# Retention block and gated MLP in one kernel: residual of all pairs through DMA transposes, small work moved to VectorE and GpSimd, and another written order

## The chip, the core and the metric

The kernel runs on one core of a Trainium2 chip. The metric is the device time of one launch in microseconds. The kernel before took 213.18 us, the median of three runs (212.71 to 213.91). One more execution was taken by the hardware profiler; its numbers are below.

## The reference

Two blocks, one after the other, for a batch of 8 sequences of 576 positions.

```
# 1: retention, 8 heads of 64
scores = (q @ k.T) / sqrt(64)
ret    = scores * Dmat            # Dmat[h,i,j] = gamma[h]**(i-j) for i >= j, else 0
x      = ret @ v                  # heads side by side: x is (8, 576, 512)
# 2: gated MLP
h      = gelu_tanh(x @ w_in)      # 512 -> 1024
u, vv  = h[..., :512], h[..., 512:]
v_n    = (vv - mean) / sqrt(var + 1e-6) * g_ln
v_s    = einsum('ts,bsd->btd', w_sg, v_n) + b_sg[:, None]
out    = x + (u * v_s) @ w_out    # fp32
```

Inputs and outputs are fp32; the kernel computes in bf16 with fp32 sums.

## The kernel before

Two sequences make a pair, and there are four pairs (p = 0 to 3). The 1152 rows of a pair are nine tiles of 128 rows, numbered i = 9p + m; the middle one (m = 4) holds the last 64 rows of both sequences. Retention works in five blocks per pair, b = 5p + n: four of 256 rows of one sequence and one of the 64 + 64 last rows.

For each block, q, k and v are loaded as fp32 (lines 338 and 341). q and v are multiplied by powers of gamma and cast to bf16 (line 384, tiles `qb`, `vb`); k is cast only (lines 372 and 374, `kb`). q and k are transposed on TensorE against the identity, either 128 rows wide (line 420) or as two concurrent 64-row halves (line 430), and copied out of PSUM (lines 253 and 254, `qT`, `kT`). In the last pair the q and k of the four 256-row blocks are transposed by four DMAs instead (line 455). Scores are matmuls (line 486), masked on VectorE while they leave PSUM (lines 499 and 502, `ret`). The state of earlier blocks is a sum of k-v products (`zp`, line 522; `run` and `zb`, lines 547 to 556). The output (line 568) lands transposed, as x's columns, in `xT`, copied there by ScalarE or VectorE (lines 253 and 254).

The MLP takes `xT` as its weights or its moving operand. Per tile: `hv` (four matmuls, line 642), gelu on ScalarE (line 649, `vg`), mean and variance on VectorE (lines 657 and 658), then four small GpSimd operations in `m_rs` (lines 662 to 665: add epsilon, power -1/2, product with the mean, sign), then the norm on ScalarE (line 677, `vn`; line 674 for the middle tile, which is written in two halves to `vmid`). `hu` (line 692) and its gelu (line 703, `uT`) need only `xT`. For each sequence, `wp` (line 713) multiplies four column groups of `vn` with the transposed w_sg (ten matmuls each), and VectorE multiplies the result into `uT` (line 723). Finally `op` (line 745) multiplies `uT` with w_out, the residual is added, and the 128 rows are stored (lines 771 and 774).

The residual x has to be in row order, but `xT` holds columns. The constant XP = 1 says which pairs do what: for p < XP, four more matmuls of `xT` against the identity go into the same PSUM tile ahead of the product (line 740), and ScalarE copies the sum out (line 760). For p >= XP, a DMA transpose on SP's queue writes the rows to `xr` (line 754; five buffers), and VectorE adds it while it evacuates (line 762).

Nothing is scheduled by the machine or by a planner: every piece of work is a job with a number, and the string ORDER lists all jobs. The program is emitted in that order, so each engine's queue is the list filtered by its engine. Job numbers follow from the loops that create the jobs; a letter after a number picks another engine (P, D, A, G; F is the wide form of the transposes). A token f16, f12 or f4 adds that many 128-column matmuls on a zero tile `warm`, merged into calls of up to 512 columns, at the head of the next PSUM tile (line 231). There are eight such tokens, 76 units, all in the first seventh of the list. All loads, stores and DMA transposes are issued by SP in list order, and SP waits at an entry whose source or buffer isn't ready; there are eight `ld` buffers and two of `ldq`.

The first jobs on each engine: TensorE turns the small vectors into columns (line 780), does f16, block 0's transposes, two groups of row transposes (line 803), f12, block 0's scores and state, f12, block 1's transposes, f4, block 0's output, block 1's scores, f4, `hv` of tiles 0 and 1, f12. VectorE scales block 0's q, does the column arithmetic (lines 784 to 796) and the copy of block 0's transposes; GpSimd sets zeros (lines 813 to 819), then scales block 0's v, block 1's q and block 1's v; ScalarE casts block 0's k. The halves of w_in are cast one each on ScalarE and VectorE.

Of the kernel before, what the change touches and what calls it, by code (L numbers as in the profile page):

```python
# [11 lines left out]
F32 = mybir.dt.float32  # L12
# [32 lines left out]
)  # L45


ENGINE = dict(P="PE", D="DVE", A="ACT", G="POOL", S="SP", F="FULL")


class Buf:
    def __init__(self, tag):
        self.tag, self.users, self.pos = tag, [], None


class Job:
# [46 lines left out]
def kernel(  # L103
# [12 lines left out]
    nc = tc.nc  # L116
# [185 lines left out]
    def wo_load():  # L302
# [6 lines left out]
        def g(c):  # L309
            nc.scalar.mul(w_out[:, c, :], wst["in", 0][:, c, :DM], col[:, c:c + 1])  # L310
# [818 lines left out]
```

## Time and profile before

| | before |
|---|---|
| median of three runs | 213.18 us |
| the profiled execution | 213.89 us |
| its span (first to last instruction) | 212.2 us |
| TensorE busy | 191.0 us, 90% |
| VectorE busy | 164.1 us, 77% |
| ScalarE busy | 118.2 us, 56% |
| GpSimd busy | 101.2 us, 48% |
| DMA | 48.6 MB, queue 1 takes 85.6% of 16 engines' span |

Busy time is the union of an engine's instruction spans. TensorE's matmuls overlap in the array, so a group's summed busy time can exceed what it adds to the chain of waits. PE is TensorE, PEld its weight loads, DVE VectorE, ACT ScalarE, POOL GpSimd and SP the engine that issues the DMAs. The chain of waits goes back from the last instruction, at each step to what released it. A row of the timeline gives start, duration, engine, line and operation.

### The profile page before, as it was taken

The numbers are of one execution on the slowest core, as the hardware profiler recorded it, in microseconds if no ns is written. First come the engines' busy times: TensorE is split into PE (matmuls) and PEld (weight loads), VectorE is DVE, ScalarE is ACT, GpSimd is POOL, SyncE is SP. The second block draws the span as 40 slices with busy tenths as digits, with TensorE's granted clock in tenths as the row PEclk, the third lists the DMA queues.
The fourth block names the chain that finished last, engine by engine and source line by source line (L and its number), as shares of the span: only waits on it lengthen the run. The fifth ranks groups of instructions, "written<-read, shape, count | busy, mean of one in ns | idle before, by whom it ended". The sixth has DMA issues, their size and how long they took to land.

```text
span 212.2 us, 7452 instructions
## 1 busy us (share of the span) xinstructions
PE 191.0 (90%) x3164; PEld 131.3 (62%) x3193; DVE 164.1 (77%) x301; ACT 118.2 (56%) x204; POOL 101.2 (48%) x155
## 2 busy tenths in 40 slices
PE   0967897998999899999999999999998999999991
PEld 0634575666866766767777757667756665576650
DVE  3679979967887977969978789789787877775572
ACT  5135687978876156749695645572744363545100
POOL 8970088269447309652398888567223212022000
PEclk9999999999999999999999999999999999999999
DMA  6999999955991988999999299959997546453696
GB/s 177 347 392 379 301 221 365 331 208 153 325 334 58 298 244 232 300 232 281 250 270 303 51 195 284 191 145 222 265 222 178 129 128 198 104 186 88 176 197 200
DMA packets 86132, 48.59 MB, mean 229 GB/s; under 512 B 37130, under 2 KB 79442, under 8 KB 86098
## 3 DMA queue, kind: packets, MB, share of 16 engines
q1 hardware_dynamic: 86080, 48.10, 85.6%
q8 instruction: 25, 0.41, 0.7%
q14 instruction: 9, 0.07, 0.1%
q10 hardware_dynamic: 18, 0.00, 0.0%
HBM read 32.94 MB, written 9.44 MB: 200 GB/s over the span
## 4 chain that ended last, share of the span: by engine, by line
PE 62%; DMA 10%; DVE 7%; POOL 7%; issue 4%; ACT 4%; SPq 3%; DVEq 0%; ACTq 0%; POOLq 0%
PE wp L713 13%; PE hv L642 11%; PE hu L692 10%; PE op L745 9%; PE pp L420 6%; PE pp L568 5%; DMA kT<-kb 4%; PE pp L486 3%; POOL vb L384 2%; DMA ld<-in_k_dram 2%; DVE ret L499 2%; SPq L455 2%; PE pp L231 2%; POOL mv L663 2%; DMA rsrc<-in_moe_b_sg_dram 2%
## 5 line engine op out<-in xcount | busy, mean ns | idle before, releaser
L499 DVE TENSOR_TENSOR ret<-pp,msk 128x1024 bf16<-128x1024 f32 x32 | 38.6, 1215 | 6.0 <-PE pp L486 5.9
L713 PE MATMUL wp<-wT,vn 128*128 128x288 bf16 x256 | 36.8, 286 | 1.0 <-DVE zb L550 0.9
L384 POOL TENSOR_TENSOR vb<-ld,gpow 128x1024 bf16<-128x1024 f32 (+1 forms) x18 | 31.6, 1759 | 12.7 <-DMA ld<-in_v_dram 7.0
L642 PE MATMUL hv<-w_in,xT 128*128 128x512 bf16 x130 | 35.3, 379 | 1.7 <-ACT xT L253 0.7
L692 PE MATMUL hu<-xT,w_in 128*128 128x256 bf16 (+1 forms) x320 | 36.0, 262 | 0.2 <-DVE xT L254 0.2
L662 POOL TENSOR_SCALAR mv<-mv 128x2 f32<-128x2 f32 (+1 forms) x20 | 5.3, 265 | 63.3 <-DVE mv L658 60.4
L745 PE MATMUL op<-w_out,uT 128*128 128x512 bf16 (+1 forms) x133 | 34.1, 373 | 0.8
L649 ACT ACTIVATE vg<-hv 128x512 f32<-128x512 f32 x36 | 21.4, 596 | 22.8 <-PE hv L642 16.1
L723 DVE TENSOR_TENSOR uT<-wp,uT 128x288 bf16<-128x288 f32 x64 | 26.3, 447 | 8.3 <-PE wp L713 8.3
L692 PEld LDWEIGHTS <-w_in 128*128 128x128 bf16 x320 | 27.8, 98 | 6.2 <-issue 0.6
L713 PEld LDWEIGHTS <-vn 128*128 128x128 bf16 x256 | 24.4, 98 | 8.8 <-issue 1.4
L703 ACT ACTIVATE uT<-hu 128x512 bf16<-128x512 f32 x36 | 21.4, 595 | 14.9 <-PE hu L692 14.7
L657 DVE BATCH_NORM_STATS2 bst<-vg 128x6 f32<-128x512 f32 x36 | 24.7, 685 | 4.6 <-ACT vg L649 4.5
L677 ACT ACTIVATE vn<-vg,mv 128x512 bf16<-128x512 f32 x32 | 25.1, 806 | 3.3 <-POOL mv L665 3.3
L253 ACT ACTIVATE xT<-pp 128x512 bf16<-128x512 f32 (+1 forms) x32 | 16.7, 547 | 18.3 <-PE pp L568 15.3
L762 DVE TENSOR_TENSOR ob<-op,xr 128x512 f32<-128x512 f32 (+1 forms) x28 | 18.4, 669 | 6.0 <-PE op L745 5.0
L745 PEld LDWEIGHTS <-uT 128*128 128x128 bf16 x148 | 13.7, 98 | 12.9 <-DVE uT L723 0.7
L642 PEld LDWEIGHTS <-xT 128*128 128x128 bf16 x144 | 13.3, 98 | 13.5 <-ACT xT L253 1.7
L384 POOL TENSOR_TENSOR qb<-ldq,gpow 128x1024 bf16<-128x1024 f32 x9 | 17.1, 1901 | 3.5 <-PE pp L568 2.4
L663 POOL TENSOR_TENSOR mv<-mv,mhalf 128x2 f32<-128x2 f32 (+1 forms) x20 | 14.5, 725 | 1.7
L713 PE MATMUL wp<-wT,vmid 128*128 128x288 bf16 x64 | 13.1, 286 | 0.0
L486 PE MATMUL pp<-qT,kT 64*64 64x128 bf16 x448 | 11.1, 219 | 1.7 <-DMA kT<-kb 0.7
(111 smaller groups left out, 266.2 us busy)
## 6 DMA issues: line engine op xcount, KB each, us to landing
ld<-in_k_dram SPq DMA_DIRECT2D x16, 512.0 KB, 6.2
ld<-in_v_dram SPq DMA_DIRECT2D x16, 512.0 KB, 5.7
out_dram<-ob SPq DMA_DIRECT2D x31, 256.0 KB, 2.5
ldq<-in_q_dram SPq DMA_DIRECT2D x7, 1024.0 KB, 8.3
out_dram<-ob SPq DMA_DIRECT2D x10, 128.0 KB, 3.3
xT<-in_moe_w_sg_dram SPq DMA_DIRECT2D x2, 576.0 KB, 5.6
ld<-in_q_dram SPq DMA_DIRECT2D x2, 512.0 KB, 4.9
xT<-in_moe_w_in_dram SPq DMA_DIRECT2D x1, 1024.0 KB
```

Of the source, the lines that this page charges most:

```text
L384: ve.tensor_tensor(dst, src, g.unsqueeze(len(src.shape) - 1).to_broadcast(list(src.shape)), op=Alu.mult)
L499: ins = nc.vector.tensor_tensor(ret[:].rearrange("p r (k t) -> p (r k) t", k=2), sc[:].rearrange("p r (k t) -> p (r k) t", k=2), (msk2 if ...
L642: ins = nc.tensor.matmul(hv[:], xTs[p][:, m, kk, :], w_in[:, kk, F2:], start=(kk == 0), stop=(kk == KK - 1))
L649: unfence(nc.scalar.activation(vgs[i][:], cur.pop(("hv", i))[:], Act.Gelu_apprx_tanh), ("V", i))
L657: nc.vector.bn_stats(bst[:], vgs[i][:])
L663: nc.gpsimd.tensor_tensor(mv[:, :w, 2], mv[:, :w, 2], mhalf[:, :w], op=Alu.pow)
L677: nc.scalar.activation(vn[:], vg[:], Act.Identity, scale=mv[:, s, 2:3], bias=mv[:, s, 3:4])
L692: ins = nc.tensor.matmul(hu[:, n, :], w_in[:, kk, 128 * c:128 * c + 128], xTs[p][:, m:m + w, kk, :], start=(kk == 0), stop=(kk == KK - 1), ...
L703: unfence(nc.scalar.activation(uTs[p][:, c0:c1, 128 * m:128 * m + 128 * w], hu, Act.Gelu_apprx_tanh), ("U", i, half))
L713: ins = nc.tensor.matmul(ps[half][:], vns[NT * p + tile_of(e, j)][e][:, 128 * c:128 * c + 128], wT[e][j][:, lo:lo + HS], start=(j == 0), s ...
L723: ins = nc.vector.tensor_tensor(uTs[p][:, c, col:col + HS], cur.pop(("wp", b, c, half))[:], uTs[p][:, c, col:col + HS], op=Alu.mult)
L745: ins = nc.tensor.matmul(op[:], uTs[p][:, c, r], w_out[:, c, cs], start=(p >= XP and c == 0), stop=(c == KK - 1), skip_group_check=True)
```

## The change

XP goes from 1 to 0: the nine tiles of the first pair no longer take the identity matmuls and the ScalarE copy, but a DMA transpose and VectorE's addition, like the others. Nine jobs (`m_X`) are added on SP.

In `m_rs`, epsilon and the sign of the mean move to two small VectorE operations at the end of `m_stats`; GpSimd keeps the power and one product. The norm, the copy of the state to bf16 (`a_Zev`), the casts of w_out, and the placing of small rows in `vmid` and `wT` may now be given to another engine by a letter in ORDER. The zeros and rows of `vmid` become two jobs each, one per buffer. Code for a finer split of a block's loads (`SPLIT`) is added, but the tuple is empty, so none of it runs.

ORDER is rewritten. All f tokens are gone. Counted from the list, before and after:

| work | before | after |
|---|---|---|
| norms | 36 ScalarE | 21 ScalarE, 5 VectorE, 10 GpSimd |
| last evacuation (`ob`) | 9 ScalarE, 28 VectorE | 37 VectorE |
| state copies (`zb`) | 24 ScalarE | 14 ScalarE, 6 VectorE, 4 GpSimd |
| evacuations of q/k transposes | 1 ScalarE, 15 VectorE | 10 ScalarE, 6 VectorE |
| k casts | 7 ScalarE, 4 VectorE, 9 GpSimd | 3, 2, 15 |
| q scalings | 6 VectorE, 14 GpSimd | 5, 15 |
| v scalings | 2 VectorE, 18 GpSimd | 1, 19 |
| casts of w_in, w_sg, w_out | 7 ScalarE, 2 VectorE, 4 GpSimd | 5, 2, 6 |
| q transposes in 64-row form | 1 | 2 |
| DMA transposes to `xr` | 27 | 36 |

At the start, block 0's k cast goes to GpSimd, block 1's q scaling to VectorE and its k cast to GpSimd, the copy of its transposes to ScalarE; one half of each w_in cast goes to GpSimd. TensorE does block 0's transposes, scores and state, then block 1's transposes before block 0's output, both scores of block 1 and block 2's q transposes before the first `hv`. At the end, the output of tile 28 comes after the last `wp` group instead of ahead of it. On SP the six loads of blocks 0 and 1 keep their order; then q of block 2 comes ahead of the first half of w_in.

```diff
 ORDER = (
-    "2 3 4 8 95 75 9 0 f16 1 77 76 96 10 98F 97 78 99 80 f12 5 14 193 191 100 194 263 11 81 f12 83 101D 192 103F 15 265 104 f4 102 268 264 195 269 196 270 "
...
+    "2 3 4 8 97 9 75 0 98G 10 1 78 77 100F 99 14 101 5 102D 15 195 265 25 196 193 103 81 194 104 105F 266 267D 11 106A 268 270 107D 287 79 271 108 272 199 "
...
-    XP = 1
+    XP = 0
...
+    SPLIT = ()
...
-        def g(c):
-            nc.scalar.mul(w_out[:, c, :], wst["in", 0][:, c, :DM], col[:, c:c + 1])
+        def g(c, eng):
+            if eng == "ACT":
+                nc.scalar.mul(w_out[:, c, :], wst["in", 0][:, c, :DM], col[:, c:c + 1])
+            else:
+                (nc.vector if eng == "DVE" else nc.gpsimd).tensor_scalar(w_out[:, c, :], wst["in", 0][:, c, :DM], col[:, c:c + 1], None, op0=Alu.mult)
...
-    def a_Zev(b, c):
+    def a_Zev(b, c, eng):
         if (b % NBK, c) in ZFIRST:
-            z_read(nc.scalar.activation(new_zb(b, c), cur["zp", b, c][:], Act.Copy), b)
+            z_read(copy(eng, new_zb(b, c), cur["zp", b, c][:]), b)
         else:
-            nc.scalar.activation(new_zb(b, c), cur["run", b, c][:], Act.Copy)
+            copy(eng, new_zb(b, c), cur["run", b, c][:])
...
-    def m_stats(i, first, slot):
+    def m_stats(i, first, slot, last):
...
         nc.vector.bn_aggr(mv[:, slot, 0:2], bst[:])
+        if last:
+            nc.vector.tensor_scalar(mv[:, :slot + 1, 1], mv[:, :slot + 1, 1], 1e-6, None, op0=Alu.add)
+            nc.vector.tensor_scalar(mv[:, :slot + 1, 3], mv[:, :slot + 1, 0], -1.0, None, op0=Alu.mult)
...
     def m_rs(i, w):
         mv = mvs[i][0]
-        nc.gpsimd.tensor_scalar(mv[:, :w, 2], mv[:, :w, 1], 1e-6, None, op0=Alu.add)
-        nc.gpsimd.tensor_tensor(mv[:, :w, 2], mv[:, :w, 2], mhalf[:, :w], op=Alu.pow)
-        nc.gpsimd.tensor_tensor(mv[:, :w, 3], mv[:, :w, 0], mv[:, :w, 2], op=Alu.mult)
-        nc.gpsimd.tensor_scalar(mv[:, :w, 3], mv[:, :w, 3], -1.0, None, op0=Alu.mult)
+        nc.gpsimd.tensor_tensor(mv[:, :w, 2], mv[:, :w, 1], mhalf[:, :w], op=Alu.pow)
+        nc.gpsimd.tensor_tensor(mv[:, :w, 3], mv[:, :w, 3], mv[:, :w, 2], op=Alu.mult)
 
-    def m_norm(i):
+    def m_norm(i, eng):
...
+        def f(dst, r):
+            if eng == "ACT":
+                nc.scalar.activation(dst, vg[r, :], Act.Identity, scale=mv[r, s, 2:3], bias=mv[r, s, 3:4])
+            else:
+                (nc.vector if eng == "DVE" else nc.gpsimd).tensor_scalar(dst, vg[r, :], mv[r, s, 0:1], mv[r, s, 2:3], op0=Alu.subtract, op1=Alu.mult)
...
-    def zero_vmid():
-        for t in vmid:
-            nc.gpsimd.memset(t[0][NB0:, :], 0.0)
-            nc.gpsimd.memset(t[1][:NB0, :], 0.0)
+    def zero_vmid(i):
+        nc.gpsimd.memset(vmid[i][0][NB0:, :], 0.0)
+        nc.gpsimd.memset(vmid[i][1][:NB0, :], 0.0)
```

More of the change, by code (lines that the diff above doesn't have):

```diff
@@ L326, in half_of, with a_load @@
         return b % NBK % 2
-    def a_load(b, t):
+    def a_load(b, t, g=None):
         p, n = divmod(b, NBK)
@@ L332, in a_load @@
         sup = t == "q" and not joint(b)
+        if g is not None:
+            if g == 0:
+                st[b, t] = new("ld", [128, H, 2 * D], F32)
+            e, r0 = ch[0]
+            for c in range(2):
+                h = slice(KK * c + 2 * g, KK * c + 2 * g + 2)
+                nc.sync.dma_start(st[b, t][:, h, :], src[2 * p + e, h, r0:r0 + 256, :].rearrange("h (p s) d -> p h (s d)", s=2))
+            return
         f_ = new("ldq", [128, H, 4 * D], F32) if sup else new("ld", [128, H, 2 * D], F32)
@@ L367, in a_prep @@
             g = powers(NQ, 3, 2)[:, n % 2 if ns == 2 else 2, :, :ns]
+            if c is not None:
+                h = slice(KK * c, KK * c + KK)
+                dst, src, g = dst[:, h], src[:, h], g[:, h]
         elif t == "k":
@@ L434, in a_T, with a_T2, a_T2ev @@
         fence(ins, ("T", b, t))
+    def a_T2(b, g):
+        tp = psum(psD, [128, 8, 2, 64], BF, "tp", "d")
+        st[b, "tp", g] = tp
+        for x in range(8):
+            ins = nc.tensor.transpose(tp[:, x].rearrange("p r i -> p (r i)"), (qb_of(b), kb_of(b))[x // 4][:, 2 * g + x // 2 % 2, x % 2].rearrange("p c d -> p (c d)"), ident[:])
+            if x == 0:
+                mark(ins, ("T2", b, g))
+        fence(ins, ("T2", b, g))
+    def a_T2ev(b, g, eng):
+        if ("qT", unit(b)) not in st:
+            st["qT", unit(b)] = new("qT", [128, 2048], BF)
+        dst = st["qT", unit(b)][:].rearrange("p (r g x i) -> p r g x i", r=2, g=2, x=8)[:, :, g]
+        unfence(copy(eng, dst, st.pop((b, "tp", g))[:].rearrange("p x r i -> p r x i")), ("T2", b, g))
     def new_T(b, t):
@@ L858, in loads @@
             B_ld[b, t] = Buf("ldq" if sup else "ld")
+            if b in SPLIT and t != "v":
+                for g in range(2):
+                    J["ld", b, t, g] = add("SP", 1100.0, T0[b] - 30000.0, lambda b=b, t=t, g=g: a_load(b, t, g),
+                                           new=None if g else B_ld[b, t], uses=[B_ld[b, t]] if g else [], nbytes=262144, run=512, parts=2,
+                                           deps=[J["ld", b, t, 0]] if g else [])
+                continue
             J["ld", b, t] = add("SP", 550.0 * (3 - ns), T0[b] - 30000.0, lambda b=b, t=t: a_load(b, t),
@@ L878 @@
     j_z0 = add("DVE", 250.0, -6e5, zero_wnat, what="zero")
-    j_z1 = add("POOL", 1700.0, -6e5, zero_vmid, what="zero")
+    j_z1 = [add("POOL", 850.0, -6e5 if not i else 40000.0, lambda i=i: zero_vmid(i), what="zero") for i in range(2)]
     j_z2 = add("POOL", 860.0, -5e5, zero_wT)
@@ L886 @@
         j_rows.append(add("DVE", 430.0, 15500.0, lambda a=a: rows(a), deps=[jb], uses=[bf]))
-    j_pv = add("ACT", 2550.0, 16000.0, place_vmid, deps=j_rows[:1] + [j_z1])
-    j_pw = add("ACT", 1600.0, 16000.0, place_wT, deps=j_rows[1:] + [j_z2])
+    j_pv = [add("ACT", 1275.0, (16000.0, 50000.0)[i], lambda eng, i=i: place_vmid(i, eng), deps=j_rows[:1] + [j_z1[i]],
+                port=True, alt=dict(ACT=1275.0, POOL=1300.0, DVE=480.0)) for i in range(2)]
+    j_pw = add("ACT", 1600.0, 16000.0, lambda eng: place_wT(eng), deps=j_rows[1:] + [j_z2], port=True, alt=dict(ACT=1600.0, POOL=1500.0, DVE=650.0))
     for j, due in zip(jv + ju, (5000.0, 5000.0, 9000.0, 9000.0)):
```

83 lines of the change are left out of this document (57 added, 26 removed), and 46 rows, old and new, of the table ORDER.

## The prediction

> **What bounds the kernel now.** I read the page's busy times first, then stretches of the span, then the chain of waits, and at the start the instructions in order of time.
>
> ```profile
> span 212.2 us, 7452 instructions
> PE 191.0 (90%) x3164; PEld 131.3 (62%) x3193; DVE 164.1 (77%) x301; ACT 118.2 (56%) x204; POOL 101.2 (48%) x155
> ...
> PEclk9999999999999999999999999999999999999999
> ```
>
> Stretches: their length, then busy us (instructions) of TensorE, weight loads, VectorE, ScalarE and GpSimd, granted clock, DMA share, GB/s.
>
> ```profile
> 0.00:20.00 20.00, 11.48 (x222) 7.04 (x223) 13.40 (x36) 7.71 (x12) 13.19 (x33) 1.00 0.97 322
> 20.00:60.00 40.00, 35.41 (x635) 25.94 (x640) 32.84 (x59) 32.43 (x55) 21.59 (x31) 1.00 0.92 278
> 60.00:160.00 100.00, 97.68 (x1836) 67.94 (x1854) 82.96 (x142) 60.45 (x110) 59.01 (x72) 1.00 0.96 228
> 160.00:200.00 40.00, 38.82 (x451) 25.78 (x441) 28.56 (x56) 17.63 (x29) 7.44 (x20) 1.00 0.55 146
> 200.00:212.20 12.20, 7.64 (x50) 4.58 (x48) 6.31 (x13) 0.00 (x0) 0.00 (x0) 1.00 0.76 194
> ```
>
> Three stages with different limits. From 60 to 200 us TensorE is idle for 2.3 + 1.2 = 3.5 us of 140: there a microsecond of its work is a microsecond of the span. From 20 to 60 us it idles 4.6 us and shares the stage with VectorE (82%) and ScalarE (81%). Before 20 us it idles 8.5 us and does filler besides:
>
> ```profile
> 0.00:20.00 20.00, 4.80 (x12) 1.19 (x12) 1.00 0.97 322
> 20.00:60.00 40.00, 2.04 (x11) 0.90 (x10) 1.00 0.92 278
> ```
>
> That is line 231 alone, the matmuls on the zero tile `warm`: 6.8 us of busy time, all before 60 us. The chain of the first 24 us:
>
> ```profile
> 5.67 1.82 PE pp L231 x4
> 7.49 1.73 PE pp L420 x16
> ...
> 10.27 1.27 PE pp L231 x3
> ...
> 13.59 1.44 DVE qb L374
> ...
> 15.08 1.08 PE pp L420 x16
> ...
> 20.13 0.38 PE hv L642
> ...
> 22.02 0.65 PE pp L231 x3
> ```
>
> Two readings. Filler stands in the chain, so TensorE's own queue is late by it. And the same work changes its price: sixteen transposes take 1.73 us at 7.5 us and 1.08 at 15; a filler matmul takes 0.42 us at 10.3 (1.27/3) and 0.22 at 22 (0.65/3). The array ran at half rate until some point between 11.5 and 15 us, though the granted clock is printed as full in every slice.
>
> **The change part by part.**
>
> *Residual of the first pair.* The 36 matmuls against the identity go. Chain of the stretch 60 to 90 us, shares by line:
>
> ```profile
> by line: PE op L745 19.4%; PE wp L713 13.1%; PE hv L642 11.3%; PE pp L420 9.5%; issue 9.4%; PE hu L692 8.0%; PE pp L568 7.6%; PE op L740 6.3%; PE pp L486 4.4%; ACT xT L253 4.0%; PE zp L522 3.4%; DVE xT L254 2.3%; DVE zb L550 1.4%; DVEq L254
> ...
> 60.00:90.00 30.00, 3.13 (x32) 2.13 (x32) 1.00 0.80 238
> ```
>
> L740 is 6.3% of 30 us = 1.9 us for 32 of the 36, so 2.1 us for all, on the bound engine. Its busy time (3.13 x 36/32 = 3.5 us) counts overlap and is the upper end; 1.9 is the lower. I take **-2.1**.
>
> *What replaces it.* Nine evacuations go from ScalarE to VectorE as additions, and nine DMA transposes enter SP's queue.
>
> ```profile
> L762 DVE TENSOR_TENSOR ob<-op,xr 128x512 f32<-128x512 f32 x26 | 17.6, 688 | 5.7 <-PE op L745 5.0 <-PE wp L713 0.3 <-issue 0.3
> ...
> L754 SPq DMA_TRANSPOSE xr<-xT x27: 1201/1270/3427, 87.7 to 202.5; - x27
> ...
> DMA to landing us min/median/max: 2.3/3.1/6.9
> ...
> SPq L774 <- ACT ob L760: 12.7, 2, 8.7
> ```
>
> VectorE: 9 x 0.69 = 6.2 us, beside its 17 idle us of 60 to 160. SP: 9 x 1.27 = 11.4 us of issuing (to 9 x 3.4 = 31 when the DMA engines are full), in the stretch where SP now waits 12.7 us for ScalarE's evacuations with later loads queued behind. So I cost it at nothing; without that cover, SP's issue would delay loads, not TensorE directly (rival three).
>
> *Filler.* Before 20 us it lies in gaps that stay gaps. After 20 us the chain holds 0.65 at 22.0; 2.04 us is the busy time of all of it. Between 0.65 and 2.0 I take **-1.2**.
>
> *One pair of transposes* in 64-row form instead of 128-row form:
>
> ```profile
> 113.99 0.57 PE pp L430 x32
> ```
>
> 0.57 for the work that took L420 1.08 at 15 us, on an array perhaps not yet at full rate (between 0 and 0.5): **-0.3**.
>
> *Norm chain and casts.* m_rs loses two of four GpSimd instructions (one rescaling of the mean and the epsilon), which go to VectorE; norms (5 to VectorE, 10 to GpSimd) and casts leave ScalarE.
>
> ```profile
> L662 POOL TENSOR_SCALAR mv<-mv 128x2 f32<-128x2 f32 (+1 forms) x20 | 5.3, 265 | 63.3 <-DVE mv L658 60.4 <-ACT kb L372 2.5
> L665 POOL TENSOR_SCALAR mv<-mv 128x2 f32<-128x2 f32 (+1 forms) x20 | 4.7, 237 | 1.7
> L374 POOL CAST qb<-ld 128x512 bf16<-128x512 f32 x1 | 0.6, 610 | 0.0
> L374 POOL CAST kb<-ld 128x1024 bf16<-128x1024 f32 x8 | 8.2, 1037 | 5.7 <-DMA ld<-in_k_dram 5.7
> L384 POOL TENSOR_TENSOR qb<-ld,gpow 128x512 bf16<-128x512 f32 x4 | 4.2, 1042 | 0.0
> L499 DVE TENSOR_TENSOR ret<-pp,msk 128x1024 bf16<-128x1024 f32 x32 | 38.6, 1215 | 6.0 <-PE pp L486 5.9
> L788 DVE TENSOR_SCALAR colt<-col 128x4 f32<-128x4 f32 x1 | 0.2, 170 | 0.0
> L254 DVE COPY kT<-pp 128x2048 bf16<-128x2048 bf16 x5 | 6.1, 1221 | 1.5 <-PE pp L420 1.4
> ```
>
> A GpSimd norm is not in the trace: between the one-input cast of its size (0.61) and the two-input product (1.04); it has one tensor input, so I take 0.65. Twelve such instructions (two tiles are split in halves) are 7.8 us (7.3 to 12.5). GpSimd: -10.0 (L662, L665) + 7.8 + six more k casts, one q and one v scaling, casts and small copies, about 15, gives 114, 55%. VectorE: +6.2, +40 small operations at no more than 0.17 = 6.8, +5 for five norms and six state copies, -14 for nine fewer evacuations of transposes (six of 1.22, three half as wide) and four fewer preparations: 168, 81%. ScalarE falls to about 103. No total reaches TensorE's; these cost **nothing** as sums, as waits up to +5 (below).
>
> *The start.* Instructions in order of time, before:
>
> ```profile
> 8.86 1.90 POOL L384 TENSOR_TENSOR vb<-ld,gpow 128x1024 bf16<-128x1024 f32 x1
> 10.72 1.90 POOL L384 TENSOR_TENSOR qb<-ld,gpow 128x1024 bf16<-128x1024 f32 x1
> 13.52 1.50 DVE L374 CAST qb<-ld 128x1024 bf16<-128x1024 f32 x1
> 19.10 1.06 ACT L253 ACTIVATE w_in<-xT 128x1024 bf16<-128x1024 f32 x1
> ```
>
> Block 1's transposes wait for its q on GpSimd (to 12.6), then its k on VectorE (to 15.0). Changed: q on VectorE right after block 0's copy (near 10.5, plus 1.3 to 1.5), k on GpSimd after block 0's v (near 10.5, plus 1.04): transposes near 12 instead of 15.1. That lead is not kept whole: half of w_in is now cast on GpSimd, behind half of a q scaling (1.9) that itself follows VectorE's half, so the first hv matmul comes near 19.9 against 20.1. What stays is work already done by then: one more transpose group (about 1), no filler in the way. Going on by the same rows to the fourth hv tile, with score tiles advanced and hu tiles put back, I come out 1.5 to 2 us ahead. VectorE (82% in 20 to 60) can eat it, and the doubled path can give more: between -4 and +3.5, I take **-1.5**.
>
> *The end.* Output tile 28 moves behind the last wp group, where TensorE now waits for VectorE's last product:
>
> ```profile
> 203.48 0.46 DVE uT L723
> ```
>
> **-0.4** (0 to 0.46); the remaining six stores keep their order.
>
> *New waits.* The whole order is another one, with norms in GpSimd's queue behind scalings of 1.9 us, and in it m_rs. The 3.5 us idle of 60 to 200 could shrink or grow; I take **+1.2** (0 to +5).
>
> Sum: 212.2 - 2.1 - 1.2 - 0.3 - 1.5 - 0.4 + 1.2 = 207.9. The profiled execution took 213.89 for its span of 212.2, so 209.6; the median shown (213.18) is 0.7 below that execution: **208.9**.
>
> **A page against it.** The Trainium skill, "TensorE: Matmul & The Clock Gate", Part 1, says that the array starts at half rate, is released after some 3.4 us of sustained activity and is throttled again after about an idle window of that length; its Part 4 adds that transposes don't count as such activity in the same way. The half-price rows above agree with the first; no row here shows a second throttling. By that page the filler was no waste, and the second rival below would be the outcome.
>
> **The rivals.**
>
> *GpSimd sets the pace (17%).* The first wp group needs the norm of tile 4, which becomes a GpSimd job.
>
> ```profile
> 47.01 1.05 POOL mv L662
> ...
> 53.47 2.56 PE wp L713 x20
> ```
>
> Already now GpSimd's m_rs stands in the chain ahead of that group. If its added 12 us lie there and at 80 to 130 us, and a third of it (4 us) shows: 207.9 + 4 = 211.9, as a run 212.9. Against it: two operations fewer in m_rs, 0.5 us a time.
>
> *The array stays slow (13%, slower than before).* Place: 12 to 30 us. Block 0's output now waits for VectorE's q scaling, two score evacuations (L499) and two small operations on the state: 10.5 + 1.3 + 2 x 1.2 = 14.2, so near 15. Without filler, nothing is ready between the transposes, done near 13, and that; to 20 us TensorE has about half its time filled. If it is at half rate when hv and hu start, what takes 8.95 us in 20 to 30
>
> ```profile
> 20.00:30.00 10.00, 8.95 (x115) 6.40 (x116) 9.31 (x17) 6.79 (x13) 2.78 (x5) 1.00 1.05 280
> ```
>
> less 0.65 filler is 8.3 us and takes 16.6; 1 us of it fits in the gaps, 7.3 don't: 207.9 + 7.3 = 215.2, as a run 216.2. It decides from the point where slow work after 20 us exceeds the 4.3 us won elsewhere; a release within 3 us leaves about 212 as a run. For it: the slow rows up to 11.5 us. Against: the rate at 15 us, reached although the chain had just been on VectorE for 1.44 us.
>
> *The transposes come late (8%).* VectorE works in order, so an xr that lands late stops everything behind the addition. At 6.9 us landing instead of 3.1 nine times, half covered: 9 x 3.8/2 = 17 us at worst; a quarter of it, 4 us, gives 213 as a run. For it: DMA share 0.96 in 60 to 160. Against: no wait of L762 on xr among the 27 made now.
>
> *The start gains its whole 4 us (10%)*: 207.9 - 2.5 = 205.4, as a run 206.4.
>
> **How the numbers follow.** The forecast has 52%, its own range 207 to 211. With the early start 62% are clearly faster; of rival one and three (25%), spread around 212.9, 6 are faster, 13 within, 6 slower; the slow array's 13% are slower. Within 0.5% (about what a measurement here can tell from no change) is 212.1 to 214.2. So faster 0.68, same 0.13, slower 0.19. The range goes from 205 (early start) to 214.5, leaving out the slow array at its full price.
>
> **What would show it.** No L231 or L740; no L760; TensorE's busy time near 180.5; idle in 60 to 200 us below 5. Right for the start: sixteen L420 transposes near 12 us and the first hv near 20. Wrong: hv groups of four taking 1.7 us instead of 0.86 after 20 us; wp waiting for vn from GpSimd; L762 waiting for xr; the forecast falls if TensorE's idle time grows by more than its work shrinks.

## The result, and the profile after

The changed kernel takes 221.06 us, the median of four runs (219.7 to 222.4), beside 213.55 us of the kernel before (four runs, 212.71 to 215.14). The ratio is 1.0371, with a 95% interval of 1.0311 to 1.0432: the change makes the kernel 3.7% slower, where 2% less was forecast. The ratios here leave out executions over 1.5% longer than the fastest one of the same kernel, the medians beside them do not, so the two can differ by about a per cent. The profiled execution took 219.91 us, with a span of 218.2.

First the page of the changed kernel: span, busy times, and the granted clock in 40 slices.

```profile
span 218.2 us, 7405 instructions
...
PE 187.8 (86%) x3124; PEld 129.4 (59%) x3151; DVE 172.2 (79%) x351; ACT 103.5 (47%) x165; POOL 134.5 (62%) x144
...
PEclk9999999999999999999979999999969999999999
```

VectorE and ScalarE come out near the forecast (168 and 103), GpSimd does not: 134.5 us, not 114. And the clock row, all nines before, now has two dips. Where the time went is read best at three marks on TensorE: the first wp, the first of the outputs behind the last wp, and the end of the span. Rows of the timeline: start, duration, engine, line, operation. Before:

```profile
53.41 1.15 PE L713 MATMUL wp<-wT,vn 128*128 128x288 bf16 x8
...
203.03 4.66 PE L745 MATMUL op<-w_out,uT 128*128 128x512 bf16 x23
```

After:

```profile
49.76 1.14 PE L758 MATMUL wp<-wT,vn 128*128 128x288 bf16 x8
...
207.62 5.35 PE L790 MATMUL op<-w_out,uT 128*128 128x512 bf16 x27
```

| | before | after | difference |
|---|---|---|---|
| start to first wp | 53.41 | 49.76 | -3.65 |
| first wp to last outputs | 149.62 | 157.86 | +8.24 |
| last outputs to the end | 9.17 | 10.58 | +1.41 |
| span | 212.2 | 218.2 | +6.0 |

So the start won even more than the forecast gave it, and the middle lost more than twice that. The weight loads ahead of the first wp are the same in both, line by line, but for the filler and for one transpose group that the changed kernel has done by then as well, so the 3.65 us are not work put off. What TensorE waited for in the middle, from the view of waits (total us, times, longest), the longest of before first, then the changed kernel:

```profile
PE wp L713 <- DVE zb L550: 0.9, 1, 0.9
...
PE wp L758 <- DVE uT L768: 3.1, 1, 3.1
...
PE pp L451 <- POOL qb L405: 2.4, 1, 2.4
...
PE wp L758 <- POOL vn L715: 1.4, 1, 1.4
PE hu L737 <- DVE ob L807: 0.9, 1, 0.9
```

From 60 to 200 us these views name 8.5 us of waits after, and 2.0 before (the wait for `vn` lies at 59 us and comes on top). Two places matter.

*104 to 109 us: GpSimd.* Its instructions ahead of block 12's q transposes:

```profile
97.60 4.25 POOL L715 TENSOR_SCALAR vmid<-vg,mv 64x512 bf16<-64x512 f32 x2
101.93 1.90 POOL L405 TENSOR_TENSOR qb<-ldq,gpow 128x1024 bf16<-128x1024 f32 x1
103.79 0.76 POOL L703 TENSOR_TENSOR mv<-mv,mhalf 128x2 f32<-128x2 f32 x1
...
104.80 2.08 POOL L715 TENSOR_SCALAR vn<-vg,mv 128x512 bf16<-128x512 f32 x1
106.84 1.91 POOL L405 TENSOR_TENSOR qb<-ldq,gpow 128x1024 bf16<-128x1024 f32 x1
```

They run without a gap, and TensorE has the last one's result at 108.8. Three norm instructions, for two tiles, take 6.3 us of the 11 (4.25 + 2.08). The groups of instructions (count, busy, mean ns of one):

```profile
L715 POOL TENSOR_SCALAR vn<-vg,mv 128x512 bf16<-128x512 f32 x8 | 16.7, 2096 | 0.0
L713 ACT ACTIVATE vn<-vg,mv 128x512 bf16<-128x512 f32 x20 | 15.8, 806 | 9.7 <-POOL mv L704 9.6
...
L715 POOL TENSOR_SCALAR vmid<-vg,mv 64x512 bf16<-64x512 f32 x4 | 9.3, 2320 | 0.2
```

A norm on GpSimd is 2.1 us, and a half tile isn't cheaper; on ScalarE it is 0.81. Twelve are 26.0 us where the prediction had 7.8. That is most of GpSimd's excess over the forecast (18.2 of 134.5 - 114 = 20.5).

*150 to 158 us: a late load.* SP issues the load of block 17's q at 147.99, where the kernel before issues it at 125.86. VectorE's scaling of it, with a product for wp behind it in the queue, stands still until 156.70. The row of SP, then the row of VectorE with the idle time before it and its cause:

```profile
147.99 1.34 SPq L351 DMA_DIRECT2D ldq<-in_q_dram  x1
...
156.70 1.23 DVE L405 TENSOR_TENSOR qb<-ldq,gpow 128x1024 bf16<-128x1024 f32 x1 [4.39 <-DMA ldq<-in_q_dram]
```

Both stalls have a second part. Stretches of 2 us: length, busy us of TensorE, weight loads, VectorE, ScalarE, GpSimd, then the granted clock.

```profile
106.00:108.00 2.00, 0.40 (x2) 0.00 (x0) 1.90 (x5) 0.75 (x2) 2.00 (x2) 1.00 0.71 161
108.00:110.00 2.00, 1.20 (x34) 1.05 (x35) 1.93 (x4) 0.12 (x1) 2.00 (x2) 0.68 0.89 179
110.00:112.00 2.00, 2.00 (x11) 1.40 (x10) 0.70 (x2) 2.00 (x2) 1.82 (x4) 0.50 0.75 169
...
156.00:158.00 2.00, 0.00 (x0) 0.00 (x0) 1.30 (x2) 0.00 (x0) 1.26 (x1) 1.00 1.44 300
...
160.00:162.00 2.00, 1.78 (x5) 0.65 (x5) 1.30 (x4) 1.39 (x3) 0.69 (x1) 0.50 0.80 222
```

Behind each idle time the clock is granted at half for a while. By stretches of 10 us:

```profile
100.00:110.00 10.00, 6.91 (x149) 4.66 (x144) 9.71 (x17) 2.11 (x5) 9.84 (x7) 0.94 0.92 191
110.00:120.00 10.00, 9.89 (x179) 7.15 (x180) 7.22 (x13) 5.87 (x8) 8.78 (x10) 0.89 1.02 240
...
160.00:170.00 10.00, 9.73 (x54) 5.81 (x55) 7.42 (x20) 4.46 (x8) 3.90 (x5) 0.83 0.94 203
```

That is 0.6 + 1.1 us at the first place and 1.7 at the second, so 3.4 us of array time lost at most, behind waits of 2.4 and 3.1 us. At half rate, 1.7 us lost are 3.4 us of lowered clock.

### The profile page after: what moved, and what is told of

Its sections match the earlier page's. It is cut to its first block, busy times and chain, and to the rows that moved or that the text cites. A ratio compares the mean times of both kernels' runs of the same rounds, so it can differ in the third digit from the quotient of the medians.

```text
span 218.2 us, 7405 instructions
## 1 busy us (share of the span) xinstructions
PE 187.8 (86%) x3124; PEld 129.4 (59%) x3151; DVE 172.2 (79%) x351; ACT 103.5 (47%) x165; POOL 134.5 (62%) x144
## 4 chain that ended last, share of the span: by engine, by line
PE 54%; DVE 21%; POOL 9%; DMA 6%; issue 4%; ACT 2%; SPq 1%; DVEq 0%; POOLq 0%
PE op L790 12%; PE wp L758 11%; PE hu L737 10%; PE hv L680 9%; DVE ret L537 5%; PE pp L606 4%; DMA ldq<-in_q_dram 4%; POOL qb L405 3%; PE pp L441 3%; DVE bst L695 3%; POOL vmid L715 2%; PE pp L524 2%; POOL vn L715 2%; DMA ld<-in_q_dram 2%; DVE ob L807 2%
## 5 line engine op out<-in xcount | busy, mean ns | idle before, releaser
L737 PE MATMUL hu<-xT,w_in 128*128 128x256 bf16 (+1 forms) x320 | 37.2, 266 | 0.9 <-DVE ob L807 0.9
L790 PE MATMUL op<-w_out,uT 128*128 128x512 bf16 (+1 forms) x136 | 36.0, 386 | 1.2 <-issue 0.5
L405 POOL TENSOR_TENSOR vb<-ld,gpow 128x1024 bf16<-128x1024 f32 (+1 forms) x19 | 33.1, 1748 | 0.6 <-DMA ld<-in_v_dram 0.5
L807 DVE TENSOR_TENSOR ob<-op,xr 128x512 f32<-128x512 f32 (+1 forms) x37 | 24.2, 670 | 6.5 <-PE op L790 5.2
L254 ACT ACTIVATE xT<-pp 128x512 bf16<-128x512 f32 (+1 forms) x31 | 15.6, 546 | 21.4 <-PE pp L606 20.2
L405 POOL TENSOR_TENSOR qb<-ldq,gpow 128x1024 bf16<-128x1024 f32 x11 | 22.1, 2015 | 5.1 <-DMA ldq<-in_q_dram 2.5
L713 ACT ACTIVATE vn<-vg,mv 128x512 bf16<-128x512 f32 x20 | 15.8, 806 | 9.7 <-POOL mv L704 9.6
L254 ACT ACTIVATE qT<-pp 128x2048 bf16<-128x2048 bf16 (+1 forms) x7 | 10.6, 1508 | 15.4 <-PE pp L441 11.6
L715 POOL TENSOR_SCALAR vn<-vg,mv 128x512 bf16<-128x512 f32 x8 | 16.7, 2096 | 0.0
L393 POOL CAST kb<-ld 128x1024 bf16<-128x1024 f32 x11 | 11.6, 1056 | 6.1 <-DMA ld<-in_k_dram 6.1
```

The costliest lines, as they stand in the source:

```text
L254: return nc.scalar.activation(dst, src, Act.Copy)
L405: ve.tensor_tensor(dst, src, g.unsqueeze(len(src.shape) - 1).to_broadcast(list(src.shape)), op=Alu.mult)
L715: (nc.vector if eng == "DVE" else nc.gpsimd).tensor_scalar(dst, vg[r, :], mv[r, s, 0:1], mv[r, s, 2:3], op0=Alu.subtract, op1=Alu.mult)
L737: ins = nc.tensor.matmul(hu[:, n, :], w_in[:, kk, 128 * c:128 * c + 128], xTs[p][:, m:m + w, kk, :], start=(kk == 0), stop=(kk == KK - 1), ...
L790: ins = nc.tensor.matmul(op[:], uTs[p][:, c, r], w_out[:, c, cs], start=(p >= XP and c == 0), stop=(c == KK - 1), skip_group_check=True)
L807: ins = nc.vector.tensor_tensor(ob[:, cs], op[:], cur["xr", i][:].rearrange("p j r -> p (j r)")[:, cs], op=Alu.add)
```

## The experiments

The theories. A: GpSimd's norms are late and stop TensorE. B: the load of block 17's q, moved back in the list, does. C: the missing filler leaves the array slow. E: at the start, VectorE is held up by GpSimd. F: a wait costs twice, because it lowers the clock. (D, inputs of the last pair that are late one behind the other, came from the first runs.) Each ratio is to the kernel before on the same chip.

**Ten norms back on ScalarE**

```diff
-... 361G ... 350G ... 485G ... 518G ... 506G ... 621G ... 663G ... 664G ... 800G ... 799G ...
+... 361 ... 350 ... 485 ... 518 ... 506 ... 621 ... 663 ... 664 ... 800 ... 799 ...
```

> The changed kernel with the ten norms that it gives to GpSimd put back on ScalarE; nothing else is changed. Theory A (GpSimd's norms, 2.08 us each and not 0.65, set the pace at 47 to 58, 97 to 109 and 198 to 203 us, and the stall at 104 to 109 also lowers the granted clock for some 4 us): GpSimd falls from 134.5 to about 108 us busy, the idle time of 100 to 110 us (3.1 us) and the dip of the granted clock behind it (1.7 us) go, and of the 1.5 us idle in 50 to 60 most: 5 to 6 us less, 215 us, and TensorE's busy time falls with it by the slow stretch. Theory B (the late load of block 17's q alone is what costs): within 1 us of the changed kernel's 221. Theory C (the missing filler): no change either. ScalarE gets 12 instructions of about 0.8 us, 9 us more, which could take back 1 us.

Measured: 215.9 us (four runs), ratio 1.0106 (0.9998 to 1.0215). GpSimd is at 109.0 us. The stretches by tens:

```profile
50.00:60.00 10.00, 9.52 (x174) 6.87 (x172) 9.32 (x19) 6.92 (x9) 7.71 (x6) 1.00 1.02 299
100.00:110.00 10.00, 9.73 (x183) 7.06 (x183) 9.12 (x21) 6.27 (x9) 6.69 (x7) 1.00 0.82 150
130.00:140.00 10.00, 5.61 (x97) 3.44 (x98) 5.41 (x14) 6.49 (x11) 6.33 (x7) 1.00 1.12 285
140.00:150.00 10.00, 9.89 (x178) 6.44 (x169) 7.85 (x12) 4.26 (x7) 1.65 (x3) 0.83 0.79 207
```

Theory A holds: the stalls at 50 to 60 and 100 to 110 us are gone, the dip behind the second too, and 2.6% of the time with them (1.0371 to 1.0106, some 5.6 us). A new one stands at 130 to 140, again with a dip behind it: 2.7 us of it are a wait for block 15's q.

**Block 17's q loaded earlier, in the changed kernel**

```diff
-... 65 621G 67 634 557 ... 191 545 66 532 ...
+... 65 621G 67 66 634 557 ... 191 545 532 ...
```

> The changed kernel with one entry of the list moved: the load of block 17's q (into the two-buffer tile ldq) goes from behind block 17's v to right behind block 17's k, so that it is issued near 126 us and not at 148. Theory B: VectorE's scaling of that q no longer stands in its queue for 4.4 us with a product for wp behind it; the 3.6 us of TensorE's idle time in 150 to 160 and the clock dip behind it (1.7 us) go: 5 us less, near 216. Theory A: the stall at 104 to 109 remains as it is, and this gives at most these 5 us; if GpSimd's lateness were the cause of the later stall as well, nothing is gained, 221. Theory C: 221.

Measured: 217.14 us, ratio 1.0117 (0.995 to 1.0284). The wait of 3.1 us for VectorE is down to 0.8, the stall at 104 to 109 is as it was, and TensorE waits 1.8 us for block 15's q. Theory B holds, some 4 us by the medians.

**Both together**

> Both edits together: the ten norms on ScalarE and block 17's q loaded early. If theories A and B are each right and independent, the gains add: 221 - 5.5 - 5 = 210 to 211, no granted clock under 0.95 in any 10 us after 20 us, and the idle time of TensorE in 60 to 200 us falls from 10.4 to below 5. If one stall only hides the other, 215 to 216. If the filler's absence costs as well, it stays above the kernel before, 214 or more.

Measured: 217.16 us, ratio 1.0184 (1.0092 to 1.0275). The gains do not add. TensorE now gets early enough to 135 us to wait there for block 15's q, by the view of waits

```profile
PE pp L524 <- DMA qT<-qb: 4.7, 1, 4.7
```

and by stretches of 10 us

```profile
130.00:140.00 10.00, 5.30 (x82) 3.47 (x84) 5.36 (x14) 4.60 (x8) 6.32 (x7) 0.95 1.12 278
140.00:150.00 10.00, 9.78 (x168) 6.41 (x160) 6.64 (x10) 3.45 (x5) 1.04 (x1) 0.71 0.78 222
```

The late norms had hidden that this q is late as well: its load is issued at 114.3 us, where the kernel before issues it at 101.6. This is theory D.

**Block 15's q early too, on top of the ten norms**

```diff
-... 57 165F ... 61 609 ... 550 172 409 ... 666 173D 650 ... 651D 176 642 ... 191 545 66 532 ...
+... 57 61 165F ... 609 ... 550 172 173D 409 ... 666 650 ... 651D 176 66 642 ... 191 545 532 ...
```

> The changed kernel with the ten norms on ScalarE and, on the loads' side, block 15's q and block 17's q earlier: the load of block 15's q goes right behind block 13's v (issued near 100 us instead of 114), VectorE's half of its scaling right behind GpSimd's half, and the load of block 17's q right behind block 15's q transpose. With both earlier edits together the array had stood idle for 4.7 us near 135 us for that q transpose, with the granted clock at 0.71 in the ten microseconds behind it. Theory D (TensorE runs into whatever q of the last pair is loaded late, and each such wait lowers the clock): the wait for qT in 130 to 140 us and the dip go, 6 to 7 us less, 210 to 211. If the transposes through the DMA engines are what is slow (10.0 us from issue to landing) and not their start, a wait of 2 us or more stays and the time is 214 or more.

Measured: 213.64 us (ten runs), ratio 1.0023 (0.9975 to 1.007). With three inputs in time (the norms, block 15's q, block 17's q) the changed kernel is as fast as the kernel before; below it is called the mended kernel. Its page:

```profile
span 211.3 us, 7439 instructions
...
PE 186.6 (88%) x3151; PEld 128.4 (61%) x3151; DVE 169.2 (80%) x351; ACT 112.4 (53%) x177; POOL 109.0 (52%) x132
...
PEclk9999999999999999999999999999999999999999
```

The largest named wait of TensorE after 60 us (total us, times, longest), and the row of VectorE behind its longer half:

```profile
PE wp L758 <- DVE ob L807: 2.0, 2, 1.6
...
144.06 0.69 DVE L807 TENSOR_TENSOR ob<-op,xr 128x512 f32<-128x512 f32 x1 [2.20 <-DMA xr<-xT]
```

No dip of the clock is left in this execution. It came out 3 us above what was expected of it, and the longest named waits now are for VectorE's addition of the residual, once because the DMA transpose it adds was 2.2 us late. At the three marks (50.14, 200.81, 211.3) it is 3.27 us ahead at the first wp, gives 1.05 back in the middle and 1.32 at the end, so most of what the start won is spent behind it.

**The kernel before without any filler, and without the last three entries**

```diff
-... f16 ... f12 ... f12 ... f4 ... f4 ... f12 ... f12 ... f4 ...
+...
```

> The kernel before with the eight filler entries taken out of its list and nothing else: the matmuls on the zero tile are gone. By the prediction's step on the filler, 1.2 us less after 20 us and nothing before 20 us: 212.3 beside 213.5. Theory C (filler holds the array at full rate; without it the matmuls of 12 to 30 us run at half rate): slower, up to 7 us, 216 to 220, with hv groups of four taking 1.7 us after 20 us. If the array is released by the real work alone, as the changed kernel's transposes at 19.8 us (1.05 us for sixteen) say, it is 211 to 213.5.

Measured: 219.61 us, ratio 1.0301 (1.0187 to 1.0415).

```profile
16.00:18.00 2.00, 1.24 (x58) 1.16 (x57) 1.58 (x3) 1.15 (x3) 0.00 (x0) 0.50 1.08 395
...
36.00:38.00 2.00, 0.00 (x0) 0.00 (x0) 0.68 (x2) 0.00 (x0) 1.47 (x3) 0.50 1.10 364
...
40.00:42.00 2.00, 1.52 (x7) 0.58 (x5) 1.56 (x2) 2.00 (x4) 0.00 (x0) 0.50 0.93 261
```

Theory C holds for the old order: where the filler stood, the clock now falls to a half, at 14 to 21 us and again at 35 to 45. All four runs have it lower on the mean of the span, 0.954 to 0.978, where the seven of the kernel before beside them have 0.989 to 1.000. In the second stretch lies a pause of 2.7 us at 35.9 us for which the profile names no cause; the clock had fallen before it, so it is not what lowered it, and it is left open.

With only the last three entries (`f12`, `f12`, `f4`) taken out:

> The kernel before without its last three filler entries (12, 12 and 4 units, those that ran after 20 us); the filler before 20 us stays. The prediction's step: 1.2 us less, near 212.3 beside 213.5. By the run without any filler, where the granted clock fell to 0.50 at 34 to 44 us, the filler at 32 and 37 us keeps the clock up: then 1 to 4 us more, 214.5 to 217.5, with granted clock below 1.00 between 30 and 46 us.

Measured: 215.86 us (four runs), ratio 1.0131 (1.0036 to 1.0225). Taking away even the 2 us of filler behind 20 us costs more than it takes out of the queue. The mean granted clock of 20 to 60 us falls to 0.91 in the profiled execution, from 1.00.

**The residual of the first pair alone, on the kernel before**

```diff
-    XP = 1
+    XP = 0
```

with nine `m_X` entries, for tiles 3, 2, 1, 0, 8, 4, 7, 5, 6, in the list of loads.

> The kernel before with one part of the change alone: the residual of the first pair by DMA transposes and VectorE's addition; the identity matmuls and ScalarE's nine copies go, nine transposes enter the list of loads (each at least 16 entries ahead of its use), and the filler and everything else stay. The prediction's step: 2.1 us less, near 211.4 beside 213.5. Theory that the transposes cost: they take 1.3 us or more each of the time in which loads are issued, 12 us in all near 60 to 90 us, so that later loads come late; then nothing is won or up to 3 us are lost, 213.5 to 216.5.

Measured: 216.25 us (four runs), ratio 1.0138 (1.0026 to 1.0249). Not the 2.1 us less of the prediction, but more. The trace names no single payer. Its clock row has a dip of its own:

```profile
PEclk9999999799999999999999999999999999999999
```

That dip is at 37 us. The first of the new transposes is issued at 51.8 us, and the named waits of TensorE at 32 to 36 us are those of the kernel before (0.45, 0.57 and 0.46 us in both), which has no dip there. So whether short gaps lower the clock can differ from one execution to the next. The dip isn't what makes this kernel longer either: two of its runs took 216.2 and 216.3 us with a granted clock of 1.00.

**The residual of the first pair put back, with the three inputs in time**

```diff
-    XP = 0
+    XP = 1
```

and the nine `m_X` entries of the first pair gone.

> The run with the norms on ScalarE and block 15's and block 17's q early (213.6 beside 213.7 of the kernel before), with the residual of the first pair put back on TensorE and ScalarE: 36 identity matmuls and nine copies, nine DMA transposes fewer. The end of the list stays as the change has it. By the prediction's step, 2.1 us longer: ratio 1.012 to the kernel before. By the runs with that part alone (1.4% slower with DMA transposes in the kernel before): the transposes cost as much as they save, ratio 0.992 to 1.003; VectorE's waits for xr, and TensorE's for ob behind them, become fewer.

Measured: 213.69 us (twelve runs), ratio 0.9977 (0.9931 to 1.0023), beside 1.0023 (0.9975 to 1.007) without. TensorE's busy time is

```profile
PE 188.3 (88%) x3187; PEld 129.9 (61%) x3187; DVE 166.7 (78%) x342; ACT 116.5 (54%) x186; POOL 108.7 (51%) x132
```

so the 36 matmuls are 1.7 us of it (188.3 - 186.6), near the 2.1 of the prediction, and the time doesn't show them. The DMA form saves them and pays them back; SP's queue, VectorE's 2.5 us more and the DMA engines can each be the payer, and these runs do not tell them apart. TensorE's waits for VectorE's addition from 60 to 200 us became fewer, as expected (one, where the mended kernel has four), but not smaller in sum (3.4 us beside 3.0), as one of the transposes left was 4.0 us late:

```profile
PE wp L758 <- DVE ob L807: 3.4, 1, 3.4
...
DVE ob L807 <- DMA xr<-xT: 4.0, 1, 4.0
```

And the clock stayed at 1.00 behind this wait of 3.4 us, longer than either of those that lowered it in the changed kernel. Idle time of this length can lower the clock, but doesn't always.

**Filler at the start of the mended kernel**

```diff
-... 98G 10 ... 102D 15 195 ...
+... 98G f16 10 ... 102D 15 f20 195 ...
```

> The run with block 15's and block 17's q early, and filler put back at the start alone: 16 units ahead of block 0's transposes and 20 ahead of its scores. Theory C (the array is still at half rate until near 16.8 us in the changed kernel, since nothing runs before 7.5 us and between 9.4 and 11.9): block 1's transposes take 1.05 us and not 1.88, TensorE is some 2 us further at the first hv, and 0 to 1.5 us of it last to the end. If VectorE and the loads set the start's pace, no change against the run without it.

Measured: 213.94 us (ten runs), ratio 1.0000 (0.9942 to 1.0058). Block 1's transposes do fall to 1.05 us, at 14.18. But the work is done sooner than VectorE brings more, and then:

```profile
16.00:18.00 2.00, 1.74 (x90) 1.52 (x91) 2.00 (x2) 1.59 (x2) 1.08 (x1) 1.00 1.09 369
18.00:20.00 2.00, 1.30 (x23) 1.14 (x23) 2.00 (x5) 1.54 (x3) 0.87 (x1) 0.66 1.21 345
20.00:22.00 2.00, 2.00 (x15) 1.44 (x13) 2.00 (x3) 1.56 (x3) 0.17 (x1) 0.50 0.90 308
```

the clock falls at 18.6 us and the first hv group begins at half (21.01 us, 2.41 us for its eight matmuls where it was 1.89).

**The end of the list as before, on the mended kernel**

```diff
-... 881 847 870 735 855 864 848 872 871 860 856 861 ... 863 850 892 868 869 874 851 893 852 875 882 876 885 883 ...
+... 881 847 850 870 735 855 851 864 848 872 871 860 856 852 861 ... 863 892 885 868 869 874 893 875 882 876 883 ...
```

> The run with the norms on ScalarE and block 15's and block 17's q early, and the end of the list as in the kernel before: the output of tile 28 ahead of the last wp group instead of behind the last four, and the last transpose for a residual (tile 35) right behind the one of tile 31 on the loads' queue. The prediction's step on the end counted the move behind wp as 0.4 us won. If that holds, taking it back costs 0.4 us, 214.0 beside 213.6. If instead seven tiles behind the last wp group with five buffers for the transposed residual hold VectorE up at the end (it stood idle for 1.04 us at 204 us), 0.5 to 1.5 us are won, 212.1 to 213.1.

Measured: 216.03 us, the median of four runs from 212.62 to 216.79, beside 214.28; no ratio can be given. In its profile the last stretch is 9.64 us and not 10.49, but TensorE paused for 2.8 us at another place without a named cause. On the whole time it is inconclusive.

On top of it the residual of the first pair was put back:

> The run with the end of the list mended, and the residual of the first pair put back on TensorE (36 matmuls against the identity) and ScalarE (nine copies); its nine DMA transposes leave the queue of loads. The prediction's step: the DMA form saves 2.1 us, so this run is 2 us longer than the one it starts from, near 215. The theory from the kernel before with that one part changed (1.4% slower with DMA transposes): the queue of loads, VectorE (80% busy) and the DMA engines (91% of their span) pay more than TensorE gains, and this run is the same or up to 2 us shorter, 211 to 213.

Measured: 214.99 us (twelve runs), ratio 0.9938 (0.9888 to 0.9989). Median (214.28 for the kernel before) and ratio point to different sides, so no verdict is drawn from it.

**The start without GpSimd's overlap, with the end of the list as before**

```diff
-... 98G ... 77 100F 99 ... 103 ...
+... 98A ... 100F 99 ... 103 77 ...
```

> The run with the end of the list mended, and two entries of the start changed: block 0's k cast on ScalarE instead of GpSimd, and GpSimd's zeros for wT behind block 1's k cast instead of ahead of block 0's v. Theory E (VectorE's small operations on the columns, 1.03 and 2.22 us for what takes 0.16 us elsewhere, stand still while GpSimd reads SBUF, and so the copy of block 0's transposes starts at 10.9 and not at 9.4 us): L834 and L841 fall to 0.2 us, the copy starts by 9.6 us, block 0's scores by 10.9 and block 1's transposes near 13 us; 0.5 to 1.3 us of it last to the end, 211.5 to 212.5. If VectorE's total sets 10 to 50 us, the first scores come earlier and the fourth hv tile does not; no change.

Measured: 214.4 us (twelve runs), ratio 1.0002 (0.9953 to 1.0052).

```profile
6.34 0.16 DVE L834 SCALAR_TENSOR_TENSOR colt<-col,colt 128x4 f32<-128x4 f32 x1
...
7.77 0.17 DVE L841 TENSOR_TENSOR col<-colr,col 128x10 bf16<-128x10 f32 x1
```

and the stretches before the first hv:

```profile
18.00:20.00 2.00, 0.56 (x18) 0.49 (x18) 2.00 (x3) 1.05 (x2) 0.93 (x1) 0.94 1.17 346
20.00:22.00 2.00, 2.00 (x17) 1.72 (x17) 2.00 (x5) 1.17 (x3) 0.18 (x2) 0.50 0.95 281
```

Theory E holds where it looks: the two operations, 1.03 and 2.21 us in the changed kernel, are 0.16 and 0.17, and block 0's scores come at 10.52 and not at 11.91, block 1's transposes at 12.79 and not at 14.18. It does not hold for the end: the 1.4 us become gaps at 17 to 20 us, the clock falls to a half, and the first hv comes at 21.52 us, later than the 20.64 without the edit.

**Filler inside one stall of the changed kernel**

```diff
-... 161 ...
+... f40 161 ...
```

> The changed kernel as it is, with filler at one place: 40 units (ten matmuls of 512 columns on the zero tile, 2.2 us at full rate) ahead of block 12's q transposes, where TensorE stood idle from 106.4 to 108.8 us for GpSimd's q scaling. GpSimd stays as late as it is; only the array isn't idle while it waits. Theory F (standing idle lowers the granted clock to 0.50 for some 3.9 us behind the wait, on top of the wait itself): the granted clock stays at 1.00 in 108 to 113 us, the eight hu matmuls behind the transposes take 1.04 us and not 1.89, and 1.5 to 1.9 us of the 221 are won, 219. If the lowered clock comes from something else (VectorE and GpSimd both busy, the DMA load), it stays, and the time is 221.

Measured: 218.95 us (four runs), ratio 1.0125 (1.0032 to 1.0219). The stretches of the stall:

```profile
106.00:108.00 2.00, 2.00 (x11) 0.91 (x10) 1.90 (x4) 0.87 (x2) 2.00 (x2) 1.00 1.06 79
108.00:110.00 2.00, 1.75 (x41) 1.07 (x39) 1.93 (x4) 0.38 (x1) 2.00 (x2) 1.00 0.73 140
110.00:112.00 2.00, 2.00 (x36) 1.52 (x37) 1.01 (x3) 1.98 (x2) 1.82 (x4) 1.00 1.00 186
```

and the hu group behind the transposes:

```profile
109.51 1.05 PE L737 MATMUL hu<-xT,w_in 128*128 128x256 bf16 x8
```

Theory F holds at this place: GpSimd is as late as ever, but the array isn't idle, the clock stays at 1.00, and the hu group takes 1.05 us where it took 1.89. It rests on one profiled execution with the filler; without it, the same stall of 2.4 us was followed by a dip in both traces that have it (the changed kernel, and the run with block 17's q early). TensorE is 1.4 us further at 114 us (an hv group at 114.29 and not 115.70). How much of it reaches the end is not settled by four runs that lie over 7 us apart; in the profiled one the other stall, at 154 to 159 us, lasted 4.9 us, and the mean clock of the span, 0.983, is no better than the 0.984 of the changed kernel.

## Why the prediction was wrong, by its own steps

*The start and the filler behind 20 us (-1.5 and -1.2).* By the first wp the changed kernel is 3.65 us ahead, the mended one 3.27: the sum of 2.7 came near, but in part by luck, as steps that led to it did not happen. Block 1's transposes came at 14.17 us, not near 12, since VectorE's small operations stood behind GpSimd, and the first hv came at 20.64, 0.5 us later than before (20.13) and not 0.2 earlier; the lead was made between there and the first wp. The Trainium skill, "SBUF — State Buffer", "Who interferes with whom", says that a VectorE operation with two SBUF inputs and a GpSimd operation that reads SBUF exclude each other for a whole instruction; L841, a difference of two SBUF tiles, agrees (2.21 us beside GpSimd's v scaling, 0.17 without it). And the filler was no waste: in the old order removing it costs 3.0%, removing only its last 2 us 1.3%. The changed kernel does without: filler put back at its start won nothing (1.0000 beside 1.0023). In its trace TensorE is at work from 11.9 to 17.8 us, block 1's transposes at 14.17 still take 1.86 us and block 2's at 19.75 take 1.05; that this stretch of work is what brings the array to full rate was not tested.

*The residual (-2.1, its replacement at nothing).* The size on TensorE was right (1.7 us), the "nothing" was not: 1.4% slower alone on the kernel before, no difference on the mended one. The cover named, ScalarE's copies that kept SP waiting, did not make the transposes free. The same passage says that SP's issue "would delay loads, not TensorE directly", and puts no price on what a late load then does to TensorE: two late loads of q cost it a wait of 3.1 us, through VectorE, and one of up to 4.7 us, through a DMA transpose of q. Whether the nine new transposes on SP are part of why these loads were late is not shown; loading both earlier in the list was enough.

*The norm chain (0.65 us, bounds 0.61 to 1.04).* This is the first step that failed. The true 2.1 us lie outside the bounds: the nearest rows by size, a cast and a product of two tensors, are not near an operation with two column scalars. GpSimd's load was missed by 20 us, and norms stood in front of its scalings; putting the ten norms back on ScalarE took some 5.6 us off.

*New waits (+1.2, 0 to +5).* This is the term that made the forecast wrong. Measured: 6.5 us more waits from 60 to 200 us, 1.4 us near 59 us, and up to 3.4 us of lowered clock. Less the identity matmuls (1.7) and the output tile that went to the end (4 x 0.22 = 0.9) that is 8.7, against the 8.24 of the table. That the two agree so well is partly chance, as the 3.4 is an upper end. Two omissions made it: no load of the last pair was followed to where the new list issues it, and a wait was priced at its own length. The prediction quoted the rule for the latter, the Trainium skill, "TensorE: Matmul & The Clock Gate", Part 1, that the array is throttled again after an idle window, and used it for the start alone. The traces agree that a stall can halve the clock, but give no fixed length: 0.50 came behind 2.4 us of idle time, and in the runs with an earlier start behind stretches in which the array was 28 to 87% busy, while 3.4 us of it in the run with the residual put back left the clock at 1.00.

*The end (-0.4).* No gain. TensorE went from the last wp straight into the outputs in the kernel before as well (the outputs begin at 203.03, 0.25 us behind the start of the last wp pair), and the view of waits names none there, so there was next to nothing to fill; one more tile stands behind it now, and the stretch is 1.41 us longer.

*What would show it.* TensorE's busy time should have been 180.5 us. The mended kernel, with no lowered clock behind the start, has 186.6. The 180.5 takes off the two lines at the busy time that each has alone (3.5 and 6.8 us), though their matmuls overlap their neighbours: with and without the 36 identity matmuls the mended kernel differs by 1.7. The trace of before also holds 29 fewer matmuls than weight loads (3164 and 3193); 14 of the 144 hv and 15 of the 148 op matmuls are missing, which makes TensorE look freer than it was. That is not much, since a record lasts 0.38 us and the next of its group begins 0.22 us later: put back where their weight loads stand, the 29 add some 1.7 us to the busy time, by estimate. The rest of the 6.1 us is open.

*The rivals.* "GpSimd sets the pace" was the right mechanism, at the place named (the first wp group and 80 to 130 us), with 4 us for what took 5.6 when taken away. "The array stays slow" did not happen where it was put, when hv and hu start (transposes at 1.05 us by 19.75), but its mechanism acted at 108 and 160 us. "The transposes come late" was seen once in the mended kernel (2.2 us) and once with the residual put back (4.0 us). No rival was a late load of q, and that was the other half: the norms and the two loads together undo the loss. Of the pairs only the norms with block 17's q was run (1.0184), so whether another two would do is open; the norms alone leave 1.0106, with an interval that overlaps that of all three.

## What to carry to other kernels

Price an operation on a new engine by a row with the same operands there, and if there is none, keep the upper bound open: the norm was three times its "nearest" row. A wait on TensorE can cost more than its length: behind waits of 2.4 and 3.1 us the lowered clock took up to 1.7 us more here, and behind one of 3.4 us nothing. In a hand-made order look what the last engine to deliver is at each such place, loads included, because taking away one wait only shows the next. Filler that looks like waste in a chain can be what holds the clock.

## What was not expected of the hardware

- A GpSimd norm with two column scalars takes 2.1 us for 128 x 512, and for half the rows no less (a mean of 2.3 over four); casts of w_out with one column scalar took 1.58 us, a plain cast of that size 0.61. The same norm takes 0.54 us on VectorE and 0.81 on ScalarE.
- VectorE operations on 4 to 10 columns took 1.03 and 2.21 us beside GpSimd work, and 0.16 and 0.17 without.
- The granted clock fell to 0.50 for 3.4 us behind a wait of 2.4 us; with ten matmuls on a zero tile in the wait it stayed at 1.00. Behind a wait of 3.4 us in another run it stayed at 1.00 without any, and in one execution of the kernel before with XP = 0 it fell at 37 us, behind gaps that left it at 1.00 in the kernel before.
- Getting the array to full rate earlier, or its inputs earlier, moved nothing that the runs can show; in both traces gaps opened behind the earlier work, and the clock was low later (0.50 at 20 to 22 us).
